# Retention and squared-ReLU feed-forward on one core: v loaded with its q and k, and chunk 8 turned by VectorE instead of TensorE

## The chip, the core and the metric

The kernel runs on one NeuronCore of one Trainium2 chip. The metric is the time of one execution on the device in microseconds (us); the number for a kernel is the median of several runs. A profile is one further execution with the hardware profiler on. PE is TensorE's matmuls, PEld its weight loads, DVE is VectorE, ACT is ScalarE, POOL is GpSimd, and SP is SyncE, whose queue issues nearly all DMAs here.

## What is computed

A retention layer (linear attention with a decay for each head) feeds a feed-forward network:

```
q, k, v: (8, 8, 576, 64)  float32            # batch, heads, sequence, head size
scores = (q @ k^T) / sqrt(64)
ret    = scores * gamma[h] ** (i - j)  for i >= j, else 0      # gamma = 1 - 2 ** (-5 - h)
attn   = ret @ v
x      = attn, as (4608, 512)                # tokens, heads * head size
h      = max(x @ w_in, 0)                    # w_in (512, 2048), float64 at the input
out    = (h * h) @ w_out                     # w_out (2048, 512), float64 at the input
```

## The kernel before

**Chunks.** The 4608 tokens are taken in 36 chunks of 128 (`C`), and four chunks make a block of 512 tokens (`TOK`). A sequence of 576 is four and a half chunks, so a chunk is handled as two halves of 64. Retention needs no full score matrix: for each half a 64 by 64 square of scores is made, and what earlier tokens add is carried in a 64 by 64 sum for each head, `u`. The decay is folded into q and v by scaling them.

**One chunk.** `load` (L140) brings q, k and v of a chunk by DMA on SP's queue, q and k in two DMAs each and v in one (twice as many where a chunk spans two sequences). The buffers are pools: q has three, k five, v four, so the DMA for a chunk has to wait until the chunk three, five or four back is no longer needed. `scale_q` (L392) and `scale_v` (L492) scale q and v in place, on GpSimd from chunk 2 on. q and k then have to be turned, so that the head dimension lies across partitions. There are two ways:

- `turn` (L456) does it on TensorE: `turn_in` makes 16 transposes (L445) into two PSUM banks of the pool `ps_f` (which has three, shared with the feed-forward steps), and `turn_out` copies the two banks to SBUF (L454), both on ScalarE when called with `(0, 0)`.
- `flip` (L412) does it on VectorE: one instruction for k and one for q (L416) turn the squares of 32 by 32, and 16 small copies, 32 by 256 each, put the squares in their places. The two instructions are put in the list `flips`, the copies in the list `moves`; `move(count)` (L428) sends the next copies that are due to ScalarE (L431), and `move(C, i)` all that are left of chunks up to i.

Chunks below `N_TURN` = 9 are turned by TensorE, the others by VectorE.

`whole(i)` (L589) does the retention of chunk i, and the scores of chunk i + 1, on TensorE in a fixed order: own values into `x_ps` (L574) beside the growth of the carry, k^T v into `u_ps` (L568); then `grown` (L500), by which ScalarE copies `u_ps` to `u_sb` (L501); scores of the next chunk (L480); the carried part (L609); then the second half of L574 and L568. The mask on the scores is VectorE's (L491). At the end `x_out` (L542) copies the result to `xT` on ScalarE (L550), and a second `grown` follows.

**Feed-forward.** Each finished block gives a list of steps. Block 0 has 16 steps `first_in` (L667), one for each piece of `w_in`: four matmuls of 512 columns (L677), a ReLU on ScalarE (L683) and, at the next step, a square on ScalarE (L685). `w_in` comes as float64 and is turned into float32 in 16 pieces just ahead of these steps: `convert(6)` (L333) issues the six instructions of one piece, five on VectorE (L227, L231, L238, L241, L244) and one on ScalarE between them (L235, after L227 and before L241). The pieces run two ahead of the steps. The later blocks have 28 steps `ffn_in` (L700), in which products of Strassen's scheme (L717) are made; the activations are stored to DRAM (L648), and after the loop over the chunks the second half of the kernel multiplies them with `w_out` (L1063).

**Order.** There is no scheduler: each engine runs its instructions in the order in which the program writes them. The loop at L915 has one round for each chunk i from 5 on:

```
move(C, i)
whole(i - 1)
if i + 1 < N_TURN: turn(i + 1, (0, 0))
scale_v(i + 1)
loads(i)                      # q and k of chunk i + 3, v of chunk i + 2
if N_TURN <= i + 2: flip(i + 2)
ffn(i - 1)                    # 3 steps while block 0 lasts (rounds 5 to 8), else 7
scale_q(...)                  # up to chunk i + 2, from round N_TURN - 3 on up to i + 3
```

In `ffn` (L813), while block 0 lasts, each of the three steps is preceded by `move(4)`, `convert(6)` and the next entry of `flips`; so k of chunk i + 2 is turned ahead of step 1, q ahead of step 2, and the copies begin in step 3 of the same round and go on in the next.

Of the kernel before, what the change touches and what calls it, by code (L numbers as in the profile page):

```python
# [41 lines left out]
def kernel(  # L42
# [48 lines left out]
    N_CH = n_tok // C  # L91
# [48 lines left out]
    def load(i, names="qkv"):  # L140
        if i == 0:
            nc.sync.dma_start(dv, decays)
        got = loaded.setdefault(i, [None] * 3)
        for name, pool, src in (("q", ld3, q), ("k", ld5, k), ("v", ld4, v)):
            if name not in names:
                continue
            t = got["qkv".index(name)] = pool.tile([128, H, D], F32, tag=name, name=f"{name}_ld")

            issue = nc.scalar if i == 0 and name != "q" else nc.sync
            b, c0 = divmod(i * C, S)  # L150
            runs = [(b, c0, slice(0, C))] if c0 + C <= S else [(b, c0, slice(0, CH)), (b + 1, 0, slice(CH, C))]
            for e in range(1 if name == "v" else 2):
                for b, c0, to in runs:
                    at = src[b, :, c0:c0 + to.stop - to.start, :].rearrange("h s d -> s h d")
                    if name == "v":
                        issue.dma_start(t[to], at)
                    else:
                        issue.dma_start(t[to, e * HP:(e + 1) * HP, :], at[:, e::2, :])
# [174 lines left out]
    def convert(count):  # L333
        for _ in range(count):
            f = next(w_in_steps, None)
            f and f()
# [55 lines left out]
    def scale_q(i, engine, parts=(slice(0, H),)):  # L392
        at = N_PAT + i % N_PAT
        for heads in parts:
            t = loaded[i][0][:, heads, :]
            engine.tensor_tensor(t, t, dv[:, heads, at:at + 1].to_broadcast(list(t.shape)), op=ALU.mult)  # L396
# [1 line left out]

    N_TURN = 9
    ps_t = [None]
    moves = []

# [7 lines left out]
    def flip(i):  # L412
        t = work2.tile([128, 4, 2, HP, 32], F32, tag="flip", name="flip")

        def one(j):
            nc.vector.transpose(t[:, :, j, :, :], loaded[i][j].rearrange("s (p e) (d a) -> s (e d) p a", e=2, d=2))  # L416

        def two():
            one(0)
            to = new_qk(i)  # L420
            for b in range(C // 32):
                for g in range(4):

                    moves.append((i, done[0] + (1 if steps[0][0] == 0 else 2), to[32 * g:32 * g + 32, :, :, 32 * b:32 * b + 32], t[32 * b:32 * b + 32, g, :, :, :]))

        flips.extend([lambda: one(1), two])

    def move(count, i=N_CH):  # L428

        while moves and count and moves[0][0] <= i and (moves[0][1] <= done[0] or count == C):  # L430
            nc.scalar.copy(*moves.pop(0)[2:])  # L431
            count -= 1
# [23 lines left out]
    def turn(i, engines=(0, 1)):  # L456
        turn_in(i)
        turn_out(i, engines)
# [338 lines left out]
    def step():  # L797
        n, f, *args = steps.pop(0)
        done[0] += 1
        f(*args)  # L800
        for _ in range(2 if len(transfers) > 2 else 1):
            if transfers and ahead[0] > QUIET:
                transfers.pop(0)[1]()
# [9 lines left out]
    def ffn(i):  # L813

        if steps and steps[0][0] == 0:

            for _ in range((N_W1 - N_EARLY) * C // TOK):
                move(4)
                convert(6)
                for f in flips[:1]:  # L820
                    f()
                del flips[:1]
                step()
            return
        count = N_MP * NP * C // TOK
        while steps and count:
            held[0] = count <= 1

            due = sum(m[0] <= i + 2 for m in moves)
            move(max(2, min(4, -(-due // (count - 1)))) if count > 1 else 0)  # L830
            ahead[0] = count
            busy[0] = len(flips) > 0
            for f in flips[:1]:
                f()
            del flips[:1]
            step()
            count -= 1
        held[0] = busy[0] = False
        ahead[0] = N_DF
# [6 lines left out]

    def loads(i):
        if i + 3 < N_CH:
            load(i + 3, "qk")
        if i + 2 < N_CH:  # L850
            load(i + 2, "v")

    halves = (slice(0, HP), slice(HP, H))
    warm(5)
# [52 lines left out]
    convert(3)  # L907
    scores(4)
    turn(5, (0, 0))
    load(7, "qk")  # L910
    scale_q(6, nc.gpsimd)
    convert(3)
    step()
# [1 line left out]
    for i in range(N_EARLY + 1, N_CH + 1):  # L915
        move(C, i)
        whole(i - 1)
        if i == N_EARLY + 1:
            convert(4)
        if i + 1 < N_TURN:  # L920
            turn(i + 1, (0, 0))
        if i + 1 < N_CH:
            scale_v(i + 1)
        loads(i)
        if N_TURN <= i + 2 < N_CH:
            flip(i + 2)
        ffn(i - 1)
        for j in range(n_scaled[0], min(i + (4 if i > N_TURN - 4 else 3), N_CH)):
            n_scaled[0] += 1
            scale_q(j, nc.gpsimd)  # L930
# [296 lines left out]
```

## Time and profile before

| | |
|---|---|
| runs | 931.31, 931.64, 931.79 us |
| median | 931.64 us |
| the profiled execution: its own time | 931.4 us |
| the profiled execution: span of its profile | 929.7 us |
| TensorE clock granted | 0.999 |
| PE matmul busy | 922.7 us, 99% of the span |
| VectorE busy | 756.2 us, 81% |
| ScalarE busy | 346.4 us, 37% |
| GpSimd busy | 84.3 us, 9% |
| copies L431, number and mean | 432, 402 ns |
| transposes of VectorE L416, number and median | 54, 702 ns |
| transposes of TensorE L445, number and median of one | 144, 222 ns |

How to read it: matmuls are pipelined and overlap, so the duration of one is not what it adds to the time; the distance between the starts of instructions tells that. The page divides the span into busy time by engine (part 1), the chain of work that ended last (part 4), groups of instructions by line (part 5) and DMA issues (part 6). In a timeline a line gives the start in us from the span's beginning, the duration in us, the engine, the line of the program, the operation, what it writes and reads, how many instructions are merged in the line, and in brackets how long the engine had been idle and what ended that. In a table of stretches a line gives the stretch, its length, and for each of PE, PEld, DVE, ACT and POOL the busy time with the number of instructions, then the granted clock, the busy share of the DMA engines and GB/s. Rounds 6, 7 and 8 of the loop at L915 begin at about 54, 67.15 and 80.41 us.

### The profile page before, as it was taken

To read this page: it belongs to the slowest core of one execution; us is meant where nothing else is said; L and a number is where in the kernel's file an instruction comes from. 1 tells how busy PE (TensorE), PEld (TensorE's weight loads), DVE (VectorE), ACT (ScalarE), POOL (GpSimd) and SP (SyncE) were. 2 spreads that over 40 slices of the span, in tenths; PEclk is the share of its full clock that TensorE was granted. 3 is DMA by queue.
4 is the path that set the end of the run, shared out by engine and by line. 5 is a ranking of instruction groups with operands and counts; after the bars stand their busy time and mean duration, and the time that the engine had idled before them with its cause. 6 is when DMAs were issued, how large, how long until landed. Compare 5 with 4: busy or idle time off the path is not lost.

```text
span 929.7 us, 21073 instructions
## 1 busy us (share of the span) xinstructions
PE 922.7 (99%) x8548; PEld 830.3 (89%) x8548; DVE 756.2 (81%) x1215; ACT 346.4 (37%) x788; POOL 84.3 (9%) x84
## 2 busy tenths in 40 slices
PE   8999999999999999999999999999999999999998
PEld 7654888888888888888888899999999999999997
DVE  5888798888898888979876587878888888877887
ACT  3457767667676676676711110000000000000000
POOL 3322111121111111211000000000000000000000
PEclk9999999999999999999999999999999999999999
DMA  9998657678666785784379996566666575465523
GB/s 223 223 258 231 169 150 200 165 212 267 166 182 182 261 216 146 224 267 140 115 255 345 381 334 194 145 165 197 175 165 195 151 209 156 116 177 138 151 85 68
DMA packets 297152, 181.29 MB, mean 195 GB/s; under 512 B 194112, under 2 KB 270016, under 8 KB 296160
## 3 DMA queue, kind: packets, MB, share of 16 engines
q1 hardware_dynamic: 292064, 178.81, 66.4%
q10 hardware_dynamic: 4928, 1.08, 0.6%
q8 instruction: 67, 1.10, 0.5%
q14 instruction: 29, 0.24, 0.1%
q0 software_dynamic: 64, 0.07, 0.0%
HBM read 109.39 MB, written 70.52 MB: 194 GB/s over the span
## 4 chain that ended last, share of the span: by engine, by line
PE 98%; DVE 1%; issue 0%; POOL 0%; ACT 0%; POOLq 0%; DVEq 0%
PE h_b L717 18%; PE o_b L1063 17%; PE h_a L717 12%; PE h_c L717 12%; PE o_c L1063 12%; PE o_a L1063 12%; PE h_ps L677 6%; PE x_ps L574 3%; PE sc_ps L480 2%; PE x_ps L609 1%; PE u_ps L568 1%; PE idle_ps L845 0%; PE t_ps L445 0%; PE sc_ps L509 0%; PE x_ps L535 0%; DVE room L513 0%
## 5 line engine op out<-in xcount | busy, mean ns | idle before, releaser
L717 PE MATMUL h_b<-room,w 128*128 128x256 f32 x768 | 181.5, 379 | 0.0
L431 ACT COPY qk<-flip 32x256 f32<-32x256 f32 x432 | 173.8, 402 | 6.7
L717 PEld LDWEIGHTS h_b<-room,w 128*128 128x128 f32 x768 | 145.8, 190 | 20.0 <-DVE room L736 0.2
L717 PE MATMUL h_a<-room,w 128*128 128x256 f32 x512 | 123.9, 385 | 0.0
L717 PE MATMUL h_c<-room,w 128*128 128x256 f32 x512 | 121.0, 379 | 0.0
L717 PEld LDWEIGHTS h_c<-room,w 128*128 128x128 f32 x512 | 97.3, 190 | 13.2
L717 PEld LDWEIGHTS h_a<-room,w 128*128 128x128 f32 x512 | 95.0, 190 | 13.7
L1063 PE MATMUL o_b<-room,w 128*128 128x192 f32 x496 | 90.7, 326 | 0.0
L1076 ACT COPY r<-o_a 128x192 f32<-128x192 f32 x28 | 8.9, 319 | 209.4 <-PE o_a L1063 209.4
L1063 PEld LDWEIGHTS o_b<-room,w 128*128 128x128 f32 x496 | 82.3, 190 | 0.0
L724 DVE SCALAR_TENSOR_TENSOR room<-room 128x512 f32<-128x512 f32 x96 | 67.2, 700 | 3.3
L396 POOL TENSOR_TENSOR q_ld<-q_ld,dv 128x512 f32<-128x512 f32 x34 | 37.8, 1113 | 286.2 <-DMA q_ld<-in_q_dram 240.7
L1063 PE MATMUL o_a<-a,w 128*128 128x192 f32 x352 | 62.6, 326 | 0.0
L1063 PE MATMUL o_b<-s,w 128*128 128x192 f32 x336 | 61.5, 326 | 0.0
L1063 PE MATMUL o_c<-s,w 128*128 128x192 f32 x336 | 61.5, 326 | 0.0
L1063 PE MATMUL o_c<-room,w 128*128 128x192 f32 x336 | 61.5, 326 | 0.0
L677 PE MATMUL h_ps<-room,w 128*128 128x512 f32 (+1 forms) x152 | 57.7, 532 | 0.6 <-DVE w L244 0.5
L1063 PEld LDWEIGHTS o_a<-a,w 128*128 128x128 f32 x352 | 58.1, 190 | 0.1
L1063 PE MATMUL o_a<-room,w 128*128 128x192 f32 x320 | 56.9, 326 | 0.0
L1063 PEld LDWEIGHTS o_b<-s,w 128*128 128x128 f32 x336 | 55.8, 190 | 0.0
L1063 PEld LDWEIGHTS o_c<-s,w 128*128 128x128 f32 x336 | 55.8, 190 | 0.0
L1063 PEld LDWEIGHTS o_c<-room,w 128*128 128x128 f32 x336 | 55.8, 190 | 0.0
(117 smaller groups left out, 1412.6 us busy)
## 6 DMA issues: line engine op xcount, KB each, us to landing
g_dram<-room SPq DMA_DIRECT2D x164, 256.0 KB, 3.8
a<-g_dram SPq DMA_DIRECT2D x30, 512.0 KB, 5.8
room<-g_dram SPq DMA_DIRECT2D x28, 512.0 KB, 5.1
w_dram<-w SPq DMA_DIRECT2D x28, 448.0 KB, 4.4
w<-w_dram SPq DMA_DIRECT2D x7, 1792.0 KB, 9.6
q_ld<-in_q_dram SPq DMA_DIRECT2D x64, 128.0 KB, 4.1
w<-in_moe_w_in_dram SPq DMA_DIRECT2D x16, 512.0 KB, 6.0
w<-in_moe_w_out_dram SPq DMA_DIRECT2D x64, 128.0 KB, 3.4
```

The source lines that it names most:

```text
L396: engine.tensor_tensor(t, t, dv[:, heads, at:at + 1].to_broadcast(list(t.shape)), op=ALU.mult)
L431: nc.scalar.copy(*moves.pop(0)[2:])
L480: nc.tensor.matmul(st[i]["sc"][e][rows(h), hp, :], lhsT=st[i]["kT"][rows(e), hp, t], rhs=st[i]["qT"][rows(e), hp, t], start=True, stop=Tru ...
L568: return [lambda hp=hp, e=e, b=b: nc.tensor.matmul(u[rows(e), hp, :], lhsT=loaded[i][1][rows(h), 2 * hp + e, :], rhs=st[i]["vs"][rows(h), ...
L574: return [lambda hp=hp, e=e, b=b: nc.tensor.matmul(x_at(hp, e, b, h), lhsT=s["vs"][rows(h), head(hp, e), :], rhs=s["ret"][rows(h), e, hp, ...
L609: m = nc.tensor.matmul(x_at(hp, e, b, h), lhsT=u[rows(e), hp, :], rhs=s["qT"][rows(e), hp, CH * h:CH * h + CH], start=clears(b, e), stop=F ...
L677: nc.tensor.matmul(p, lhsT=w[:, c, :], rhs=xT[0][:, c, :].rearrange("p (h t) -> p h t", h=2)[:, lo:hi, at[0]:at[1]], start=(c == 0), stop= ...
L717: nc.tensor.matmul(p[:, mm, :], lhsT=w[:, c, :], rhs=xs[n][right][:, c, :], start=(j in OPENS and mm == 0 and c == 0), stop=(j in CLOSES a ...
L724: nc.vector.scalar_tensor_tensor(t, t, 0.0, t, op0=ALU.max, op1=ALU.mult)
L1063: nc.tensor.matmul(p, lhsT=w_out[j][:, m, WO_SLOT[right], :], rhs=s["lefts"][left][:, m, :], start=(i in OPENS and m == 0), stop=(i in CLO ...
L1076: nc.scalar.copy(r[:, 0, LEFT], p)
```

## The change

Three numbers and two calls are changed. `N_TURN` becomes 8, so chunk 8 is no longer turned by `turn` in round 7 but by `flip` in round 6, and `scale_q` of chunk 8 is issued at the end of round 5 instead of round 6. While block 0 lasts, up to five copies of `moves` are sent ahead of each step instead of four. In the loop v of chunk i + 3 is loaded with q and k of that chunk, and v of chunk 7 is loaded ahead of the loop with its q and k. The pools are left as they are.

```diff
-    N_TURN = 9
+    N_TURN = 8
...
         if steps and steps[0][0] == 0:
 
             for _ in range((N_W1 - N_EARLY) * C // TOK):
-                move(4)
+                move(5)
                 convert(6)
                 for f in flips[:1]:
                     f()
...
     def loads(i):
         if i + 3 < N_CH:
-            load(i + 3, "qk")
-        if i + 2 < N_CH:
-            load(i + 2, "v")
+            load(i + 3)
...
     scores(4)
     turn(5, (0, 0))
-    load(7, "qk")
+    load(7)
     scale_q(6, nc.gpsimd)
     convert(3)
     step()
```

## The prediction

> **What bounds the kernel now.** I read the whole page first, then the stage tables, then the timelines of the stage that the diff touches. Parts 1 and 4 of the page:
>
> ```profile
> PE 922.7 (99%) x8548; PEld 830.3 (89%) x8548; DVE 756.2 (81%) x1215; ACT 346.4 (37%) x788; POOL 84.3 (9%) x84
> PE 98%; DVE 1%; issue 0%; POOL 0%; ACT 0%; POOLq 0%; DVEq 0%
> ```
>
> TensorE (PE) is busy 99% of 929.7 us and is 98% of the chain that ended last. So work taken off PE is worth its time, and a new wait of PE costs its time. What stands on other engines costs nothing until PE waits for it. The 37% of ScalarE (ACT) is an average, though, and the diff acts only in rounds 6 to 8 of the main loop (round i begins with whole(i-1)). Busy time by stretch, the columns PE, PEld, DVE, ACT, POOL:
>
> ```profile
> 56.65:67.15 10.50, 10.50 (x29) 4.48 (x25) 9.92 (x15) 5.90 (x11) 2.45 (x3) 1.00 0.94 247
> 69.27:69.91 0.64, 0.64 (x20) 0.57 (x17) 0.64 (x2) 0.60 (x2) 0.00 (x0) 1.00 0.80 194
> 69.91:80.41 10.50, 10.50 (x29) 4.48 (x25) 8.44 (x16) 7.42 (x15) 0.96 (x1) 1.00 0.93 274
> 82.53:93.02 10.49, 10.49 (x28) 4.48 (x24) 9.77 (x15) 9.28 (x20) 4.08 (x5) 1.00 0.86 188
> ```
>
> The first, third and fourth are the three feed-forward steps of rounds 6, 7 and 8; the second is turn(8), the 16 transposes that go away. Here ACT works 56 to 88% of the time and VectorE (DVE) 80 to 95%.
>
> The wait that matters is in whole(). After the first group of carry products (L568, into u_ps) ACT copies u_ps to u_sb (L501), and the second group adds into the same u_ps, so it may not begin before that copy ended. PE timeline, whole(4), then ACT's:
>
> ```profile
> 41.37 0.41 PE L609 MATMUL x_ps<-qk,u_sb 64*64 64x64 f32 x16
> 41.61 0.28 PE L574 MATMUL x_ps<-qk,v_ld 64*64 64x64 f32 x4
> 41.90 0.27 PE L568 MATMUL u_ps<-v_ld,k_ld 64*64 64x64 f32 x2
> ```
> ```profile
> 41.38 0.37 ACT L501 COPY u_sb<-u_ps 128x256 f32<-128x256 f32 x1
> ```
>
> L568 begins 0.15 after the copy's end (41.75). It is the same in whole(5) to whole(7): copies from 54.64, 67.91, 81.17, products at 55.16, 68.42, 81.69. There is no slack: each us by which ACT is late at L501 is a us of PE. How near ACT is already shows its timeline in step 3 of round 7, where flip(9)'s first copies stand:
>
> ```profile
> 77.08 0.60 ACT L683 ACTIVATE room<-h_ps 128x512 f32<-128x512 f32 x1 [1.65 <-PE h_ps L677]
> 77.58 1.63 ACT L431 COPY qk<-flip 32x256 f32<-32x256 f32 x4
> 79.23 0.72 ACT L235 ACTIVATE w<-w,exp_bias 128x512 uint32<-128x512 uint32 x1
> 79.86 0.61 ACT L685 ACTIVATE room<-room 128x512 f32<-128x512 f32 x1
> 80.51 0.60 ACT L683 ACTIVATE room<-h_ps 128x512 f32<-128x512 f32 x1
> 81.17 0.37 ACT L501 COPY u_sb<-u_ps 128x256 f32<-128x256 f32 x1
> ```
>
> Four copies fit: L685 begins at 79.86, L683 could follow 0.52 to 0.54 later (80.40) and starts at 80.51, when its matmuls are done. 0.1 us is left.
>
> **What the Trainium skill says.** "VectorE: DVE Perf Modes", The three transpose paths: VectorE turns only 32x32 blocks, TensorE whole tiles into PSUM. The trace agrees: a turn by VectorE is two STREAM_TRANSPOSE (702 ns each) and 16 copies L431 that set the blocks in place. "ScalarE: Activation LUTs", What ACT_TABLE_LOAD costs: 186 ns + 0.833 ns per element without pointer operands, 399 ns for 256; L431 takes 402 (four begin in 1.65, so 0.413 each in a row). "SBUF — State Buffer", Who interferes with whom: VectorE with two SBUF inputs, and GpSimd (POOL) reading SBUF, exclude each other for a whole instruction. The trace agrees (DVE, then POOL): L244 takes 1.43 here and 0.69 elsewhere.
>
> ```profile
> 65.79 1.43 DVE L244 SCALAR_TENSOR_TENSOR w<-w,w 128x512 uint32<-128x512 uint32 x1
> ```
> ```profile
> 65.61 1.06 POOL L396 TENSOR_TENSOR q_ld<-q_ld,dv 128x512 f32<-128x512 f32 x1 [7.57 <-DMA q_ld<-in_q_dram]
> ```
>
> **The change part by part.**
>
> *Transposes gone.* 16 matmuls (L445) leave PE. Each shows 0.22, but they overlap; what counts is the distance from the first to the first matmul behind them, 69.27 to 69.91: **-0.64**. whole(7) is followed by L677 with the same gap (82.32 to 82.53) that turn(8) has before it (69.06 to 69.27), so nothing else is saved. Two ACT copies L454 (70.06 to 71.02, 0.96) and two PSUM banks go too; PE waits for no bank here, so the banks bring nothing.
>
> *Added on VectorE.* Two transposes, 0.61 to 0.70 each, in steps 1 and 2 of round 6, behind the conversion of weight pieces 9 and 10. Piece 10 ended at 63.4 and is first read at 69.91; piece 11 ended at 67.2 and is read at about 73.4. 1.3 us later both are in time: 0, and if that cover failed 1.3.
>
> *Added on ACT, round 6.* move(5) puts five copies into step 3, 5 x 0.413 = 2.06, ahead of L235. They may start when L683 of step 2 is done (64.31) and q is turned. In round 7 of the kernel before, q's turn ended 7.46 after the steps began; round 6 begins at 56.65, and scale_q(8), which held up L231 there (1.28 for 0.42 at 57.04), moves some 3 us forward. So about 64.1 to 64.3. Then 64.37 + 2.06 + 0.63 (L235) + 0.54 (L685) + 0.58 (L683) = 68.2 for L501, against 67.91: **+0.3**. If the turn is as late as with that hold, +0.8.
>
> *Added on ACT, round 7.* The remaining 11 copies of chunk 8 and the first 4 of chunk 9: five per step. Start: L431 stood 3.04 after whole(7) began (83.45), so 70.19 in round 7. Step 1: 2.06 + 0.63 + 0.54 + 0.58 gives 74.0. Step 2: the same, 77.8. In step 3 one copy of chunk 8, to 78.2; then those of chunk 9 need q's turn, which is now late itself: each L235 behind five copies holds L241 and L244 (72.27, so L241 at 73.05 and k turned at 75.1; then L235 at 76.08, L241 at 76.85, q turned at 78.9). From 78.95 four copies 1.65, then 0.63 + 0.54 + 0.58: L501 at about 82.4. PE would want it at 81.17 - 0.64 = 80.53. **+1.9**; without the wait for q's turn +1.1. Behind L501 stand only ACT's own instructions; waiting for it are L568 and the whole rest of PE's queue.
>
> *Round 8.* 15 copies instead of 12, but one L235 instead of three: 15 x 0.413 + 0.63 + 3 x 1.12 = 10.2 in 10.5 of PE, and whole(8) has no such L501, since a sequence ends there. 0. From round 9 on a round has seven steps for 16 copies.
>
> *v earlier.* The bytes are the same. v of chunk 7 (issue 1.0 to 1.2 us of SP's queue) now goes ahead of pieces 8 and 9. Piece 8, issued at 44.29 and landing 5.6 later, is read at 52.33: 2.4 of slack for 1.1, so 0; if the cover were gone, 1.1 on VectorE, and PE reads the piece 4.8 after its conversion ended. From chunk 9 on v's DMA waits in SP's queue for the products of whole(i-1), as its buffer is that of v four chunks back. Behind it are stores of the steps after that whole(), which wait longer anyway, and weight fetches. SP reaches v late by itself: at 126.95 and 142.30, when the L609 of that round were at 122.44 and 136.80. 0, bounded by the 2.1 us of a whole() on SP alone. GpSimd's wait for v (75.8 us in all) goes, but PE waited for no scaled v here; what is late next on GpSimd is q, as before.
>
> *Sum.* -0.64 + 0.3 + 1.9 = +1.55. The profiled execution took 931.4 (span 929.7 and 1.7 around it), so 932.95; it stands 0.24 under the median 931.64, which I move by the same amount: **933.2**.
>
> **Rivals.** *ACT catches up*: only PE's saving shows. For it: ACT is idle 1.4 to 1.7 us before L683 in each step of rounds 6 and 7. Against: a step would hold 2.06 + 1.75 = 3.8 of ACT in PE's 3.5. Time 931.64 - 0.64 = 931.0.
> *GpSimd holds VectorE ahead of q's turn in round 7* (or in round 6, at 0.5): one hold costs 0.74 to 0.86 (1.43 for 0.69, 1.28 for 0.42), and by the L416-L431-L501 path all of it reaches PE. For it: scale_q and scale_v come as loads land, q of chunk 10 at 79.4, within 1.3 us of q's turn, and VectorE is 95% busy in round 6. Against: in the kernel before none fell there in round 7. With one hold in each, -0.64 + 0.8 + 2.7 = +2.9, so 934.5; one in round 7 alone, +2.4, already passes 0.2%.
> *v does harm or good by itself*: PE's waits contain no v but one of 0.5 at the start, so 931.64 if it were all. That the transposes do not leave PE is excluded: its instruction list is shorter by those 16.
>
> **How the numbers follow.** Forecast 0.6 (own range 932.4 to 934.0), ACT catches up 0.12, hold 0.25, rest 0.03. 0.2% is 1.86 us, about what a measurement of this kernel can tell from no change, so "same" reaches to 933.5. A third of the forecast's own range lies above that (0.2), with the hold 0.45 slower; faster 0.03; same 0.52. Range 930.9 (PE's saving alone) to 934.8 (holds).
>
> **What would show it.** Right: L501 of whole(7) starts about 82.4 and L568 0.15 after its end; PE idle 0.3 in whole(6) and near 1.9 in whole(7), none elsewhere; no L677 waiting for a piece. Wrong: L501 at 80.5 with PE not idle, PE waiting for a conversion or a landing, or a loss after 95 us.

## The result and the profile after

| | before | after |
|---|---|---|
| median, 11 runs each | 931.28 us (931.07 to 931.83) | 933.57 us (933.12 to 937.34) |
| ratio, 95% interval | | 1.0027 (1.0019 to 1.0035) |
| the profiled execution: its own time | 931.4 us | 933.12 us |
| the profiled execution: span of its profile | 929.7 us | 931.4 us |

The changed kernel is 2.29 us slower by the medians and 1.7 us by the two spans. The profiled execution of after is the fastest of its 11. Beside later experiments the kernel was measured once more: 933.54 us (10 runs) against 931.64, ratio 1.0023 (1.0015 to 1.0032).

Parts 1 and 4 of the page of after:

```profile
PE 922.7 (99%) x8532; PEld 829.9 (89%) x8532; DVE 763.8 (82%) x1217; ACT 351.4 (38%) x802; POOL 85.6 (9%) x84
...
PE 96%; DMA 2%; DVE 1%; POOL 1%; issue 0%; SPq 0%; POOLq 0%; DVEq 0%
```

PE lost its 16 matmuls, ACT has 16 copies more and two fewer, VectorE two transposes more. VectorE's busy time, though, rose by 7.6 us, where two transposes are 1.4; most of the rest is instructions that took longer beside GpSimd, as is shown below. Note "DMA 2%" in the chain, which had none before; it is explained below.

Busy time by stretch (PE, PEld, DVE, ACT, POOL): the steps of rounds 6 and 7 of after.

```profile
56.65:67.15 10.50, 10.50 (x32) 4.57 (x28) 8.46 (x16) 7.42 (x16) 0.33 (x1) 1.00 1.05 280
69.81:80.02 10.21, 10.21 (x24) 4.19 (x24) 8.02 (x16) 9.27 (x21) 0.57 (x1) 1.00 0.92 263
```

ACT went from 5.90 to 7.42 in round 6 and from 7.42 in 10.50 us to 9.27 in 10.21 us in round 7: 91%. Step 3 of round 7, ACT's timeline of after:

```profile
77.56 0.58 ACT L683 ACTIVATE room<-h_ps 128x512 f32<-128x512 f32 x1
78.16 0.40 ACT L431 COPY qk<-flip 32x256 f32<-32x256 f32 x1
79.23 1.65 ACT L431 COPY qk<-flip 32x256 f32<-32x256 f32 x4 [0.67 <-DVE flip L416]
80.91 0.72 ACT L235 ACTIVATE w<-w,exp_bias 128x512 uint32<-128x512 uint32 x1
81.54 0.61 ACT L685 ACTIVATE room<-room 128x512 f32<-128x512 f32 x1
82.06 0.58 ACT L683 ACTIVATE room<-h_ps 128x512 f32<-128x512 f32 x1
82.53 0.36 ACT L501 COPY u_sb<-u_ps 128x256 f32<-128x256 f32 x1
```

No instruction here waits for PE any more: before, L683 had 1.65 us of idle time ahead of it and L501 came at 81.17. The one idle stretch, 0.67, is the wait for q of chunk 9 to be turned. VectorE's timeline of after shows why that is late:

```profile
77.16 0.69 DVE L241 SCALAR_TENSOR_TENSOR w<-w,w 128x512 f32<-128x512 f32 x1 [0.43 <-ACT w L235]
77.88 0.69 DVE L244 SCALAR_TENSOR_TENSOR w<-w,w 128x512 uint32<-128x512 uint32 x1
78.50 0.70 DVE L416 STREAM_TRANSPOSE flip<-q_ld 128x512 f32<-128x512 f32 x1
```

VectorE waits for ACT's L235 (76.41), which stands behind the five copies of step 2, and then ACT waits for VectorE's transpose. What PE makes of it, timeline of after:

```profile
81.25 0.28 PE L574 MATMUL x_ps<-qk,v_ld 64*64 64x64 f32 x4
82.99 0.27 PE L568 MATMUL u_ps<-v_ld,k_ld 64*64 64x64 f32 x2 [1.46 <-POOL q_ld L396]
```

PE is idle 1.46 us at L568. L501 ended at 82.89 and L568 starts 0.10 later. The releaser named in the bracket is another, GpSimd's scaling of q of chunk 10, which ended in this idle time, at 82.49 (81.43 + 1.06):

```profile
81.43 1.06 POOL L396 TENSOR_TENSOR q_ld<-q_ld,dv 128x512 f32<-128x512 f32 x1 [11.05 <-DMA q_ld<-in_q_dram]
```

The program has no such dependency: L568 reads v and k, and this v (chunk 7) had been scaled by 56.97. This wrong name is also what puts "DMA 2%" and "POOL 1%" into the chain. The experiments below show it twice more.

Comparing each matmul's start in after with its start in before tells where the 1.7 us arise; I call a change of this difference a shift, and give the place where it arises: +0.17 at 9 us (the start of the kernel, different in every execution), -0.55 at 70 us (+0.10 in whole(6), -0.64 from the transposes), +1.70 at 82 us, +0.40 at 435 us. Nothing else is over 0.1.

### The profile page after: what moved, and what is told of

The parts are those of the page before. It is cut to its first block, busy times and chain, and to the rows that moved or that the text cites. A ratio compares the mean times of both kernels' runs of the same rounds, so it can differ in the third digit from the quotient of the medians.

```text
span 931.4 us, 21033 instructions
## 1 busy us (share of the span) xinstructions
PE 922.7 (99%) x8532; PEld 829.9 (89%) x8532; DVE 763.8 (82%) x1217; ACT 351.4 (38%) x802; POOL 85.6 (9%) x84
## 4 chain that ended last, share of the span: by engine, by line
PE 96%; DMA 2%; DVE 1%; POOL 1%; issue 0%; SPq 0%; POOLq 0%; DVEq 0%
PE h_b L717 18%; PE o_b L1061 17%; PE h_a L717 12%; PE o_c L1061 12%; PE o_a L1061 12%; PE h_c L717 12%; PE h_ps L677 5%; PE x_ps L574 3%; DMA q_ld<-in_q_dram 2%; PE sc_ps L480 2%; PE x_ps L609 1%; PE u_ps L568 1%; PE sc_ps L509 0%; PE t_ps L445 0%; PE x_ps L535 0%; POOL q_ld L396 0%
## 5 line engine op out<-in xcount | busy, mean ns | idle before, releaser
L431 ACT COPY qk<-flip 32x256 f32<-32x256 f32 x448 | 180.3, 402 | 7.6 <-DVE flip L416 0.7
```

## The experiments

**Theory.** The loss at 82 us is ACT's: the copies do not fit ahead of L501 in round 7, and the late turn of q adds to it. **Rivals.** GpSimd, which the profile names at L568, is the cause; or the loads cost something by themselves, which the 0.40 at 435 us and the 0.6 us that the medians show above the spans would fit.

### Each half alone

The loads alone (`e1_v_alone`: before with the edits of the diff at `loads` and at `load(7)`) and the turn alone (`e2_turn_alone`: before with `N_TURN = 8` and `move(5)`).

> The loads alone: v of chunk i + 3 with its q and k, chunk 8 still turned by TensorE. If the loss is the small copies that hold back ScalarE's L501 in round 7 (copies theory), this is within 0.3 us of the kernel before and L501 of round 8's whole(7) stays at 81.2. If the loss comes from loads that land later and hold GpSimd, as the releaser of L568 in the changed kernel's profile (q_ld L396) says (loads theory), most of the 2.3 us shows here.

> Chunk 8 turned by VectorE and five copies a step, v loaded as before. Copies theory: TensorE waits 1.7 us at L568 in whole(7) as in the changed kernel, -0.64 + 0.1 to 0.3 + 1.7, so +1.2 to +1.4 us, and what is missing to 2.3 belongs to the loads. Loads theory: no wait there, -0.6 to 0 us.

| against before, 931.65 (70 runs) | median | ratio, interval |
|---|---|---|
| e1_v_alone (21 runs) | 933.20 | 1.0018 (1.0011 to 1.0024) |
| e2_turn_alone (18 runs) | 933.03 | 1.0017 (1.0010 to 1.0024) |

The turn alone has the shifts +0.19 at 69 us (whole(6)), -0.64 at 70 us and +1.70 at 82 us, and none later. The loads are not in it, and in this trace GpSimd scales q of chunk 10 at 79.63 to 80.69, over 2 us ahead of L568. So GpSimd's late q is not the cause.

The loads alone are no neutral edit: +1.55 us, with L501 of whole(7) in time. Its trace has +0.57 at 55 us and then +0.23, +0.42 and +0.31 at 378, 392 and 435 us. GpSimd's waits for v went, as foreseen; the waits of before, then of e1_v_alone (us in total, times, longest):

```profile
POOL v_ld L495 <- DMA v_ld<-in_v_dram: 75.8, 36, 11.1
```
```profile
POOL v_ld L495 <- DMA v_ld<-in_v_dram: 17.9, 7, 5.0
```

With v there early, GpSimd no longer pauses between the two scalings. At 373 us of before, then of e1_v_alone:

```profile
373.48 1.06 POOL L396 TENSOR_TENSOR q_ld<-q_ld,dv 128x512 f32<-128x512 f32 x1 [12.03 <-DMA q_ld<-in_q_dram]
377.52 1.54 POOL L495 TENSOR_TENSOR v_ld<-v_ld,dv 128x512 f32<-128x512 f32 x1 [2.98 <-DMA v_ld<-in_v_dram]
```
```profile
374.52 1.43 POOL L396 TENSOR_TENSOR q_ld<-q_ld,dv 128x512 f32<-128x512 f32 x1 [13.99 <-DVE room L731]
375.91 1.50 POOL L495 TENSOR_TENSOR v_ld<-v_ld,dv 128x512 f32<-128x512 f32 x1
```

So VectorE is held twice in a row, and its next result comes late for PE. VectorE's, then PE's weight loads' timeline of e1_v_alone:

```profile
374.95 1.55 DVE L637 TENSOR_TENSOR room<-room 128x512 f32<-128x512 f32 x1
376.42 1.28 DVE L264 TENSOR_TENSOR w<-w 128x256 f32<-128x256 f32 x1
```
```profile
378.82 1.59 PEld L717 LDWEIGHTS h_b<-room,w 128*128 128x128 f32 x8 [0.33 <-DVE room L736]
```

In before the same two take 0.68 and 0.41. There too VectorE was held twice, but once ahead of L736 and once behind it, and PE did not wait for L736. VectorE's timeline of before:

```profile
373.88 1.21 DVE L244 SCALAR_TENSOR_TENSOR w<-w,w 128x512 uint32<-128x512 uint32 x1
...
376.72 0.69 DVE L736 TENSOR_TENSOR room<-h_b,room 128x512 f32<-128x512 f32 x1 [0.24 <-PE h_b L717]
...
378.06 1.55 DVE L638 TENSOR_TENSOR room<-room 128x512 f32<-128x512 f32 x1
```

"SBUF — State Buffer", Who interferes with whom, of the Trainium skill states the rule behind it: a VectorE instruction with two SBUF inputs and a GpSimd one that reads SBUF exclude each other, and the one issued first blocks the other; a VectorE instruction with at most one SBUF input does not collide, outside its two-port modes. The traces agree. L637 took 1.54 to 1.55 in the four cases of this trace, in all of which GpSimd had started first; at 202.22 of before L637 and GpSimd's L495 start together, L637 takes 0.68 and L495 1.59 instead of 1.06. L731, one of whose inputs is in PSUM, took 0.67 to 0.69 in all its 18 overlaps. After 42 us GpSimd starts one scaling within 0.1 us of the last one's end 2 times in before, 28 times in e1_v_alone and 29 times in the changed kernel, of about 59 scalings each.

Two scalings without a pause are not the only way to this wait, though. e4_copies_twice, an experiment of the next section, loads v as before. At 280 us, long after the copies that it adds, its two scalings stand 1.09 us apart, both of the holds fall ahead of the same L736, and PE waits. GpSimd's, VectorE's, then PE's weight loads' timeline of e4_copies_twice:

```profile
275.79 1.06 POOL L396 TENSOR_TENSOR q_ld<-q_ld,dv 128x512 f32<-128x512 f32 x1 [10.50 <-DVE room L729]
277.94 1.10 POOL L495 TENSOR_TENSOR v_ld<-v_ld,dv 128x512 f32<-128x512 f32 x1 [1.09 <-DMA v_ld<-in_v_dram]
```
```profile
276.22 1.18 DVE L238 SCALAR_TENSOR_TENSOR w<-w,w 128x512 f32<-128x512 uint32 x1
...
278.16 1.43 DVE L244 SCALAR_TENSOR_TENSOR w<-w,w 128x512 uint32<-128x512 uint32 x1
```
```profile
280.24 0.94 PEld L717 LDWEIGHTS h_b<-room,w 128*128 128x128 f32 x5 [0.65 <-DVE room L736]
```

In the 14 traces of this case PE's weight loads wait for L736 by more than 0.3 us 21 times between 95 and 450 us. Ahead of each of them VectorE was held at least twice within 6 us. In 16 of them the scalings are at most 0.11 us apart: these are in the eight traces of kernels whose v is loaded or issued earlier. In the other five they are 1.0 to 1.1 apart: these are in the six traces of kernels with v as before. So what makes PE wait is two holds ahead of one L736, and with scalings in a row that came more often. Not every such row makes PE wait: e1_v_alone has 28 of them and three waits of this size.

### Fewer and more copies ahead of L501

`e3_copies_later` is the changed kernel with one copy in step 3 of round 7 and six in step 3 of round 8. `e4_copies_twice` is the kernel before with the four copies of step 3 of round 7 made twice.

```diff
# e3_copies_later
-                move(5)
+                move({(6, 2): 1, (7, 2): 6}.get((i, at_step), 5))
# e4_copies_twice
+                again = list(moves[:4]) if (i, at_step) == (6, 2) else []
                 move(4)
+                for m in again:
+                    nc.scalar.copy(*m[2:])
```

> The changed kernel, but step 3 of round 7 sends one copy (the last of chunk 8) instead of five, and step 3 of round 8 sends six. The loads and GpSimd's work are those of the changed kernel. Copies theory: without four copies (1.65 us) and the wait for q's turn (0.67), L501 of whole(7) starts at 80.6 to 80.9, TensorE waits there at most 0.2, and the kernel is 1.5 to 1.7 us faster than the changed one, near -0.5 us of the kernel before plus what the loads cost. Loads theory: L568 still waits until 83.0 and the time stays at that of the changed kernel.

> The kernel before, in which the four copies of step 3 of round 7 are made twice over (same source, same place). Nothing else differs. Copies theory: 4 x 0.413 = 1.65 us more on ScalarE against 0.1 us of slack, so L501 of whole(7) at 82.7 and +1.55 us. Loads theory, or slack on ScalarE that the timeline does not show: 0 to +0.5 us.

| against before, 931.65 | median | ratio, interval | shift at 82 us |
|---|---|---|---|
| e3_copies_later (21 runs) | 932.52 | 1.0012 (1.0005 to 1.0018) | +0.34 |
| e4_copies_twice (21 runs) | 933.02 | 1.0015 (1.0008 to 1.0021) | +1.44 |

Taking four copies away, and with them their wait for q's turn, removes 1.36 of the 1.70, with the loads as in the changed kernel; adding four to the kernel before makes the same kind of wait, with v loaded and chunk 8 turned as before. The 0.34 that is left has a cause of its own: L235 of step 3, no longer behind the copies, waits 0.99 us for VectorE's L227, which stands behind q's late turn. By the medians, each against before beside it, e3_copies_later is 1.0 to 1.4 us faster than the changed kernel, where 1.5 to 1.7 was expected. The copies cost there, in ACT's timeline of e4_copies_twice (the second line is the repeated ones):

```profile
78.23 1.69 ACT L431 COPY qk<-flip 32x256 f32<-32x256 f32 x4
79.94 1.69 ACT L821 COPY qk<-flip 32x256 f32<-32x256 f32 x4
...
83.27 0.36 ACT L501 COPY u_sb<-u_ps 128x256 f32<-128x256 f32 x1
```

The copies' part is shown by that. The profiled execution of e3_copies_later was the slowest of its runs (935.03), with shifts of about +1.4 at 28 us, +0.65 at 55 us and +0.41 at 68 us, ahead of its edit, so its span is no measure, only its step at 82 us. That of e4_copies_twice is the second slowest of its 21. It has +0.42 at 55 us too, without any change of loads before it: there a q landed late, was scaled at 48.48 instead of 47.16, and held L244 (1.43 at 48.93), after which the next pieces' L235 were late. It has another +0.37 between 47 and 51 us, also ahead of its edit, and the +0.43 at 278 us whose lines stand above. So round 5 is close to the edge, and no single shift at 55 us or after 95 us convicts the loads; the medians have to.

### Other orders of the turn

`e5_both_turned_first` is before with `N_TURN = 8`, four copies a step and both transposes of chunk 8 ahead of step 1 of round 6. `e7_turn_four` is before with only `N_TURN = 8`.

```diff
# e5_both_turned_first
+                at_once = 2 if i == N_EARLY + 1 else 1
-                for f in flips[:1]:
+                for f in flips[:at_once]:
                     f()
-                del flips[:1]
+                del flips[:at_once]
```

> Chunk 8 turned by VectorE with v loaded as before and four copies a step; k and q of chunk 8 are both turned ahead of step 1 of round 6, so its copies fill ScalarE's idle time in steps 2 and 3 of round 6 and 1 and 2 of round 7, and those of chunk 9 stand where they stood. Copies theory: a step holds 1.65 + 0.63 + 0.54 + 0.58 = 3.4 of ScalarE in TensorE's 3.5, no wait at L568 over 0.2 us, so TensorE's 0.64 shows: -0.3 to -0.6 us against the kernel before. If turning by VectorE costs by VectorE's load as well, 0 to +1 us.

> Only N_TURN = 8: v as before, four copies a step, q turned ahead of step 2. Copies theory: round 7 has four copies a step and no wait for q's turn, so L501 of whole(7) is late by 0.2 at most; but the last four copies of chunk 9 are left for the start of round 9, and its scores wait for them: 1.5 to 1.7 us at whole(8). In all -0.64 + 0.2 + 1.6, about +1.2 us, the wait moved from L568 in whole(7) to L480 in whole(8).

| against before, 931.74 (50 runs) | median | ratio, interval | shifts |
|---|---|---|---|
| e5_both_turned_first (13 runs) | 932.41 | 1.0005 (0.9997 to 1.0013) | +0.46 at 68, -0.64 at 70, +0.92 at 82, +0.36 at 336 us |
| e7_turn_four (14 runs) | 934.36 | 1.0023 (1.0015 to 1.0031) | -0.64 at 70, +1.92 at 93 us |

I expected a gain from the first, and it did not come. With four copies a step ACT keeps up until it stands before q's transpose, which is as late as ever. ACT's timeline of e5_both_turned_first:

```profile
77.53 0.57 ACT L683 ACTIVATE room<-h_ps 128x512 f32<-128x512 f32 x1
79.28 1.65 ACT L431 COPY qk<-flip 32x256 f32<-32x256 f32 x4 [1.17 <-DVE flip L416]
...
82.58 0.36 ACT L501 COPY u_sb<-u_ps 128x256 f32<-128x256 f32 x1
```

ACT has nothing else to do for 1.17 us, and L501 is as late as in the changed kernel. So the number of copies is not all: that L235 stands behind them, and q's transpose behind L235's piece, is a second limit. This led to the two kernels at the end. PE's wait at L568 is here put down to yet another instruction, the scaling of a v (L495).

In e7_turn_four the copies of chunk 9 end after the steps of round 8, and PE waits in whole(8) for them. PE's waits, e7_turn_four:

```profile
PE sc_ps L480 <- ACT qk L431: 1.3, 2, 0.8
```

The place is as expected; 1.92 less 0.64 is 1.28, near the +1.2 of the expectation, but the medians say +2.6. The rest is not located: its profiled execution (933.5, the sixth from below of 14) has +0.9 up to 43 us, ahead of its edit.

### The loads taken apart

`e8_v_issued_first`: before, with v still two chunks ahead, but from round 9 on issued ahead of q and k. `e9_v_scaled_apart`: v three ahead as changed, but from round 9 on `scale_v` is made to wait for the matmuls of the fourth of the seven steps and `scale_q` stands right behind the loads. `e12_v_from_round_10`: before with v three ahead only from round 10.

```diff
# e8_v_issued_first
     def loads(i):
+        if i > 2 * N_EARLY and i + 2 < N_CH:
+            load(i + 2, "v")
         if i + 3 < N_CH:
             load(i + 3, "qk")
-        if i + 2 < N_CH:
+        if i <= 2 * N_EARLY and i + 2 < N_CH:
# e12_v_from_round_10
+        if i == 2 * N_EARLY + 2:
+            load(i + 2, "v")
-            load(i + 3, "qk")
-        if i + 2 < N_CH:
+            load(i + 3, "qk" if i < 2 * N_EARLY + 2 else "qkv")
+        if i < 2 * N_EARLY + 2:
```

> The kernel before; from round 9 on v of chunk i + 2 is issued ahead of q and k of chunk i + 3, still two chunks ahead. So v has landed when GpSimd has scaled q, and GpSimd's two multiplications follow each other without the 1 to 3 us between them, as when v is loaded three chunks ahead. If the loads' cost is this pairing (VectorE held twice in a row, then late with a sum that TensorE's next product waits for), +0.5 to +1.0 us, with TensorE waiting for L736 in some rounds. If it is v's buffer or SP's queue, 0.

> The loads of the changed kernel alone (v three chunks ahead), but from round 9 on q is scaled when it lands and v is scaled only after the fourth step's matmuls, so GpSimd's two multiplications stand apart. Pairing theory: the steps of 0.2 to 0.5 us after 370 us in the trace of the loads alone go; what is left is the 0.6 us in round 6: +0.5 to +0.8 against the kernel before, instead of +1.55. If pairing is not the cause, +1.5.

> The kernel before, with v loaded three chunks ahead only from round 10 on, so that block 0 and its conversions are untouched. If the loads cost by two causes, the late L501 at 55 us (0.6) and the paired scaling on GpSimd later on (about 0.9), only the second is left: 0.8 to 1.0 us slower than before, no shift at 55 us, shifts at 278, 378 to 393 and 435 us. If the loads' cost is all at 55 us, no difference from before.

| | median, before beside it | ratio, interval | scalings back to back after 42 us |
|---|---|---|---|
| e8_v_issued_first (21 runs) | 933.15, 931.74 | 1.0014 (1.0008 to 1.0021) | 25 of 59 |
| e9_v_scaled_apart (13 runs) | 932.44, 931.74 | 1.0006 (0.9998 to 1.0014) | 9 of 59 |
| e12_v_from_round_10 (13 runs) | 932.37, 931.64 | 1.0006 (0.9999 to 1.0014) | 25 of 59 |

The first makes the pairs with v still two chunks ahead, and PE waits at the same instruction, longest at 279 us; PE's waits, e8_v_issued_first:

```profile
PE h_b L717 <- DVE room L736: 0.5, 1, 0.5
```

It costs 1.41, more than expected. Its shifts after 95 us, +0.28 at 135, +0.15 at 207, +0.69 at 278 and +0.27 at 378 us, come to 1.39. In each of the three waits over 0.3 us two holds stand ahead of L736. The edit also changes the order of the loads on SP's queue; whether that moves the holds as well is not separated from the pairs.

The second takes most pairs away and costs 0.70, 0.85 less than the loads alone, with +0.50 at 55 us left, as expected; but steps of 0.15 to 0.26 at 279, 336 and 394 us are left too, where those after 370 us were expected to go. The third keeps pairs after round 10 and costs 0.73, a little under the expected 0.8, without a shift at 55 us; of the late shifts that were expected its trace has only the one at 435 us (+0.27).

So the medians fit a split in which about half of the 1.55 arises in the first rounds and about half in the later ones. They don't show it: the intervals of the last two reach to no change, and that of the loads alone overlaps both. What is shown is that issuing v ahead, which makes the pairs, costs time though v is loaded no chunk earlier (the first). What I can't give is a price of one pair: the first and the third differ twofold with 25 each. It matters which of VectorE's instructions is hit and how soon PE needs the result, and the shifts change from execution to execution.

### The conversion ahead of the copies

`e11_convert_first` is the changed kernel with two lines exchanged. `e10_best` has the same exchange, four copies a step, both transposes of chunk 8 ahead of step 1 of round 6 (the diff of e5_both_turned_first), and v loaded as before. `after_again` is the changed kernel.

```diff
# e11_convert_first (e10_best with move(4))
-                move(5)
                 convert(6)
+                move(5)
```

> The changed kernel with the conversion of the weight piece written ahead of the copies in each step. The wait for the turn of q of chunk 9 (0.67 us of ScalarE) should go, three steps with five copies each should still leave ScalarE late: L501 of whole(7) at about 81.6 to 81.9 instead of 82.53, the shift at 82 us 1.0 to 1.1 instead of 1.7, and 0.6 to 0.7 us faster than the changed kernel. If q's turn is not held by L235, no difference.

> Chunk 8 is turned by VectorE, both of its transposes stand ahead of step 1 of round 6, four copies a step, and each weight piece is converted ahead of the copies, so that L235 no longer stands behind them; v is loaded as before. If the loss of the changed kernel at 82 us is ScalarE's copies and the late turn of q of chunk 9 behind L235, both are gone: the copy L501 of whole(7) begins at about 80.5 to 80.9, L568 waits at most 0.4 for it, and the saving of the transposes shows: 0.2 to 0.6 us faster than before. If copies ahead of L235 are not what delays it, L501 stays at about 82.4 and the kernel is 1 us slower than before.

> The changed kernel once more, beside the three others on one chip: 2.0 to 2.6 us slower than before, shifts of -0.64 at 70 us and +1.7 at 82 us as in its first profile.

| against before, 931.64 (32 runs) | median | ratio, interval | shift at 82 us |
|---|---|---|---|
| e10_best (13 runs) | 931.53 | 0.9998 (0.9990 to 1.0006) | none |
| e11_convert_first (6 runs) | 934.85 | 1.0039 (1.0027 to 1.0051) | +1.19 |
| after_again (10 runs) | 933.54 | 1.0023 (1.0015 to 1.0032) | +1.70 |

At 82 us both do what the theory says. In e11_convert_first the wait for q's turn is gone and ACT is late by its own work alone: from 70.37 to the end of L501 its timeline shows no idle time. ACT's, GpSimd's, then PE's timeline:

```profile
79.24 2.07 ACT L431 COPY qk<-flip 32x256 f32<-32x256 f32 x5
81.33 0.63 ACT L685 ACTIVATE room<-room 128x512 f32<-128x512 f32 x1
81.87 0.58 ACT L683 ACTIVATE room<-h_ps 128x512 f32<-128x512 f32 x1
82.35 0.36 ACT L501 COPY u_sb<-u_ps 128x256 f32<-128x256 f32 x1
```
```profile
80.14 1.51 POOL L495 TENSOR_TENSOR v_ld<-v_ld,dv 128x512 f32<-128x512 f32 x1
```
```profile
82.81 0.27 PE L568 MATMUL u_ps<-v_ld,k_ld 64*64 64x64 f32 x2 [0.96 <-issue]
```

GpSimd had ended both of its scalings here by 81.64, and PE waits all the same, until 0.10 after L501's end: that settles who is waited for. L501 came at 82.35, not at the 81.6 to 81.9 that I expected, in part because PE and ACT reached round 7 later (see whole(6) below). As a whole the kernel is slower than the changed one, where I expected 0.6 to 0.7 less. The profiled execution, the second lowest of six, shows two places where time is lost. One is whole(6), +0.45 at 68 us where the changed kernel has +0.10: with the conversion first, L235 of step 3 of round 6 waits for VectorE's L227, which stands behind q's turn, and the copies and L501 follow it (68.49 instead of 68.17). ACT's timeline of e11_convert_first:

```profile
64.77 0.72 ACT L235 ACTIVATE w<-w,exp_bias 128x512 uint32<-128x512 uint32 x1 [0.24 <-DVE w L227]
```

The other is +1.03 at 435 us, behind three scalings in a row. VectorE's timeline of e11_convert_first:

```profile
432.41 1.51 DVE L244 SCALAR_TENSOR_TENSOR w<-w,w 128x512 uint32<-128x512 uint32 x1
433.85 1.54 DVE L637 TENSOR_TENSOR room<-room 128x512 f32<-128x512 f32 x1
435.32 1.28 DVE L264 TENSOR_TENSOR w<-w 128x256 f32<-128x256 f32 x1
436.63 0.43 DVE L265 TENSOR_TENSOR w<-w 128x256 f32<-128x256 f32 x1
436.97 0.68 DVE L736 TENSOR_TENSOR room<-h_b,room 128x512 f32<-128x512 f32 x1
```

The changed kernel has the same row of three there, but its L244 takes 0.91; it lost 0.40. Together the two places outweigh the 0.51 gained at 82 us, by about 0.5 us; the rest of the 1.3 by which the median of only six runs is above the changed kernel's stays open.

In e10_best PE has no idle time at 82 us, although L501 comes at 81.10 and not at 80.5 to 80.9. ACT's timeline:

```profile
77.80 0.72 ACT L235 ACTIVATE w<-w,exp_bias 128x512 uint32<-128x512 uint32 x1
78.43 1.63 ACT L431 COPY qk<-flip 32x256 f32<-32x256 f32 x4
80.09 0.63 ACT L685 ACTIVATE room<-room 128x512 f32<-128x512 f32 x1
80.62 0.58 ACT L683 ACTIVATE room<-h_ps 128x512 f32<-128x512 f32 x1
81.10 0.36 ACT L501 COPY u_sb<-u_ps 128x256 f32<-128x256 f32 x1
```

But in round 6 ACT waits 0.61 us for VectorE's L227 in step 2 and then has eight copies ahead of L501 of whole(6), which begins at 68.46 and costs PE +0.40 at 68 us, against -0.64 at 70 us; +0.29 at 278 us comes on top. What is left is -0.11 by the medians, with an interval around no change, where a gain of 0.2 to 0.6 was expected. after_again has -0.64 and +1.70 at 70 and 82 us, and is +1.90 by the median, where 2.0 to 2.6 was expected. Its profiled execution, the second slowest of its ten, has +0.24, +0.46 and +0.42 at 378, 392 and 435 us, the places of e1_v_alone.

## Why the prediction was right, and where it was wrong

The time was right, 933.2 against 933.57, and so were the sign of the sum and its main term. One step failed, and that the sum came out all the same is luck: in the profile the two terms of ACT were together 0.4 too large (0.3 and 1.9 against 0.10 and 1.70), and the loads, put at 0, took just that much (0.40). The working's own sum, -0.64 + 0.3 + 1.9, is 1.56, not 1.55. The change itself was further off than the time, 1.55 against 2.29, because before stood at 931.28 in that comparison; beside later experiments it was 1.90. Of the signs of being wrong that the prediction named, one showed: a loss after 95 us.

- *Transposes gone, -0.64*: -0.64 in every kernel that has the edit. In the changed kernel's profile the shift at 70 us is -0.55, with 0.10 of it from whole(6).
- *ACT in round 6, +0.3*: L501 of whole(6) was foreseen at 68.2 and came at 68.17, but whole(6) itself began 0.16 later than before, from the start of the kernel. The term was +0.10.
- *ACT in round 7, +1.9*: L501 of whole(7) foreseen at about 82.4, measured 82.53; the wait for q's turn foreseen as about 0.7, measured 0.67. ACT and PE both reached the place 0.26 later than in the working (0.16 of start, 0.10 of whole(6)). Counted from the first copy, L501 came 12.08 us later (70.45 to 82.53) instead of 12.16, and L568 followed its end by 0.10 instead of 0.15; with the rounding of the term that is +1.70. The split into 1.1 for the copies and the rest for the turn agrees with e11_convert_first (+1.19 without the turn's wait).
- *VectorE's transposes, 0*, *round 8, 0*: no shift there in any kernel with five copies a step. With four a step (e7_turn_four) the cost moves to whole(8), 1.92.
- *"v earlier ... 0"*: wrong. Alone it costs 1.55 (interval 1.0 to 2.2). The step that failed is the sentence "GpSimd's wait for v (75.8 us in all) goes, but PE waited for no scaled v here; what is late next on GpSimd is q, as before". It asked whom GpSimd keeps waiting, and not whom it holds. The wait for v had kept the two scalings apart, by 2.98 us in the lines of 373 us; without it they come together, both of the holds fall ahead of the same L736, and PE waits for VectorE. In the first rounds it is the earlier scaling itself: that of v of chunk 7 at 49.87 us holds L238 and makes L501 late at 55 us. The working knew the hold and its size, for the rival, but looked for it at one place only.
- The sum and the parts: the profile's 1.7 is 0.17 of start, -0.64 + 0.10 + 1.70 and +0.40 from the loads. By the medians the change is +2.29 or +1.90, e2_turn_alone +1.38 and e1_v_alone +1.55, so the parts add up to more than the whole. One reason is in the traces: the changed kernel does not have the loss at 55 us (L238, 1.43), since there the program puts q of chunk 8 ahead of v of chunk 7 on GpSimd, and v's scaling comes at 55.47. Whether that holds in all executions the profiles can't tell, and the intervals of the parts (1.0 to 2.2 and 0.9 to 2.2) are wide beside the difference.

The rival "ACT catches up" is out: three steps with five copies do not fit, as its own working against it said. "GpSimd holds VectorE ahead of q's turn in round 7" did not happen in any trace with its full size; in the changed kernel L227 took 0.65 instead of 0.42 at 70.02, and VectorE waited for ACT's L235 behind it all the same. The late turn is L235's doing: with L235 ahead of the copies (e11_convert_first) q's turn ended at 77.48 instead of 79.20. The third, that v does harm or good by itself, was true, and was priced at nothing because the waits of before held no trace of it.

## What to carry over

When a wait of an engine that shares access with another goes away, ask what the wait kept apart. Two GpSimd instructions can hold VectorE twice either way; what a consumer notices is both holds ahead of the one result that it needs. A pause of 3 us kept the holds on two sides of that result here; a pause of 1.0 to 1.1 us did not always, and without a pause both fell ahead of it more often. When work moves to an engine with idle time, count that idle time ahead of the next instruction that the bound engine waits for, not over the stage. Instructions that release other engines belong ahead of the added ones, unless they have to wait themselves, as L235 did in round 6. And where the removed work is 0.64 us, 16 copies of 0.41 us need 6.6 us of room: even the best order found here gave no gain that could be measured.

## What the runs showed of the hardware

- A releaser that the profile names can be wrong: the same wait of PE for L501 was put down to GpSimd's scaling of q (after), of v (e5_both_turned_first) and to "issue" (e11_convert_first). In all three L568 begins 0.10 after L501's end; in e4_copies_twice, where L501 is the one named, it begins 0.14 after it, and in before, without idle time, 0.14 to 0.15.
- Beside GpSimd, VectorE's transposes (L416, 0.70) were not lengthened, in the five cases of before, after and e1_v_alone, nor was L731 with its input in PSUM (at most 0.69, up to 21 times a trace), while operations of one SBUF tensor with scalars were (L227, 1.28 for 0.42); "SBUF — State Buffer", Who interferes with whom, of the Trainium skill names this kind of operation among those that can enter the two-port modes and then collide; which mode L227 ran in no trace shows.
- The sum of the holds does not set the time. Counted over the VectorE instructions after 42 us that took at least 0.1 us longer than the shortest of their kind in the same trace (all of them overlap a GpSimd instruction), VectorE was held for 19.7 us in before, 26.7 in e1_v_alone and 28.7 in e9_v_scaled_apart. The last two load v alike, and the one with more holds was not the slower one by the medians (+0.70 against +1.55).
